# Order edges that hold each half piece of H behind the attention step traced before it

## The chip, the cores and the metric

The kernel runs on one core of a Trainium2 chip. The metric is the device time of one execution in microseconds (us), lower is better; times are medians of several runs, and one execution more is recorded by the profiler. Five engines run their own queues of instructions, each in order: TensorE (PE), VectorE (DVE), ScalarE (ACT), GpSimd (POOL) and SyncE (SP), which issues most DMAs. An instruction whose input or buffer is not ready holds up everything behind it on its engine.

## The reference

Three stages follow each other: attention with 32 global and 512 local tokens per batch (4 batches, 8 heads, head size 64, a window of 32 to either side, and all global tokens), a two-layer network with leaky ReLU on its 2176 rows (512 to 2048 to 512), and a soft mixture of 8 experts with 4 slots each.

```python
def _attn_ref(q_l, k_l, v_l, q_g, k_g, v_g):
    ...
    s_g = scale * np.matmul(q_g, k_all.transpose(0, 1, 3, 2))
    out_g = np.matmul(sm(s_g), v_all)
    s_ll = scale * np.matmul(q_l, k_l.transpose(0, 1, 3, 2))
    mask = np.abs(pos[:, None] - pos[None, :]) <= window
    s_ll = np.where(mask, s_ll, -1000000000.0)
    s_lg = scale * np.matmul(q_l, k_g.transpose(0, 1, 3, 2))
    s_l = np.concatenate([s_lg, s_ll], axis=-1)
    out_l = np.matmul(sm(s_l), np.concatenate([v_g, v_l], axis=2))

def _moe_ref(x, w_in, w_out):
    h = x @ w_in
    g = np.maximum(0.01 * h, h)
    return g @ w_out

def _moe2_ref(x, phi, w1, w2):
    logits = x @ phi
    d = softmax(logits, axis=0)
    slot_input = d.T @ x
    # expert e: relu(slot_input[e] @ w1[e]) @ w2[e]
    return softmax(logits, axis=1) @ slot_out
```

## The kernel before

The 2176 rows are 17 tiles of 128: tiles 0 to 15 are the local rows of the four batches, the last the global rows. Attention runs over 16 pairs of heads (batch b, pair i). A pair has these steps on PE: `a_T` turns k and q (`kTp`, `qTp`, emptied by ACT into `kT`, `qT`; DVE spreads `kT` into windows `kw`); `a_S` makes 32 score blocks `sc`, DVE adds the mask and takes maxima (`se`, `mx`, `nmx`), ACT takes eight exponentials with their sums; `a_E` turns them (`etp`, emptied by DVE into `eT`); `a_V` multiplies by the window values `vw` (`po`), and DVE writes `xn`. `g_S`, `g_E` and `g_V` (`gl`, `gg`, `get`, `geg`, `gpo`, `gxt`) do the global rows once per batch. The PSUM banks named `tp` (two) are shared by `kTp`, `qTp`, `etp`, `xtp`, `get`, `gg` and others, those named `sc` (two) by the scores.

A tile t of the network has these steps: `b_X` turns a tile of `xn` (`xtp`) into a high part `xxh` (ACT) and a rest `xxl` (DVE); `b_H` multiplies by a quarter f of `w_in` in twelve matmuls of 128x512 into a bank `hp` (two banks `hb`), which ACT empties into `g`. A half piece of H is six of the twelve. For the tiles of `BLK` (4 to 14) `blocks` then turns `g` in blocks of 32 on DVE (`gb`), and after two quarters moves 16 sub-blocks back into place: for f = 0, 1 all on POOL, for f = 2, 3 six on POOL, five on DVE and five on ACT (`MOVE`, L712). `b_M` makes logits `lg`, `b_D1` to `b_D3` the softmax pieces (`lp`, `nm`, `al`, `st`, `d`, `cm`, `ce`, `cs`, `cnat`), and `b_U` adds the slot inputs up (`up`, `uacc`; for tiles under 7 `up` sits in a bank of `hb`).

From tile 4 on, `b_items` lists the pieces of H of tile t among the later steps of tile t - 1, and `merge` deals attention's steps and these items out in proportion to the weights that stand with them. That is the order of the text. The order within an engine's queue is set by a scheduler that takes ready instructions by modelled times, so a piece of H can stand ahead of attention steps that are earlier in the text. `tc.issue_after(ins)` adds an edge of order: what the block traces on the engine of `ins` stands behind `ins` in that engine's queue. Before the change `behind` uses it for four half pieces of a tile, behind a step of the softmax (`ms["b"]`).

Of the kernel before, what the change touches and what calls it, by code (L numbers as in the profile page):

```python
# [20 lines left out]
def kernel(  # L21
# [15 lines left out]
    nc = tc.nc  # L37
# [4 lines left out]
    P = 128  # L42
# [3 lines left out]
    NQ = FF // 512  # L46
# [12 lines left out]
    def bank(tag, name, bufs):  # L59
        return ps.tile([P, 512], F32, tag=tag, name=name, bufs=bufs)  # L60

    def tp(name):
        return bank("tp", name, 2)
# [10 lines left out]
    ident = identr.bitcast(F32)  # L74
# [8 lines left out]
    def warm(t):  # L83

        nc.tensor.matmul(
            t, identr, identr.unsqueeze(1).to_broadcast([P, 4, P]), start=True, stop=True
        )
# [289 lines left out]
    xn = {}  # L377
    xb = []
    exp_last = [None]

    def a_T(b, i):
        qn, kn = nat.pop(("qn", b, i)), nat.pop(("kn", b, i))
        for src, dst, nm, bf in ((kn, kT, "kT", 4), (qn, qT, "qT", 2)):
            pt = tp(nm + "p")
            if b == 0:
                warm(pt)
            for T in range(NT):
                nc.tensor.transpose(
                    pt[:, P * T:P * T + P], src[:, T].rearrange("p h d -> p (h d)"), ident
                )  # L390
            t = sa.tile([P, S], F32, tag=nm, name=nm, bufs=bf)
            nc.scalar.activation(  # L392
                out=t, in_=pt, func=AF.Copy, scale=scale if nm == "qT" else 1.0,
            )
            dst[b, i] = t
        kt = kT[b, i]
        HW = NW // 2
        kwin[b, i] = []
        for hf in range(2):
            kw = sa.tile([P, HW, P], F32, tag="kw", name="kw", bufs=3)  # L400
            src = kt[:, 32 * HW * hf:32 * HW * hf + 96]
            src = bass.AP(src.tensor, src.offset, [src.ap[0], [32, HW], [1, 96]])
# [13 lines left out]
    def a_S(b, i):  # L416
        qt, kw = qT.pop((b, i)), kwin.pop((b, i))
        mx = sa.tile([P, 2, NT], F32, tag="mx", name="mx", bufs=2)
        nmx = sa.tile([P, 2, NT], F32, tag="nmx", name="nmx", bufs=2)
        sm = sa.tile([P, NT, 2], F32, tag="sm", name="sm", bufs=2)  # L420
        rs = sa.tile([P, NT, 2], F32, tag="rs", name="rs", bufs=2)
        es = []
        bks = [bank("sc", f"sc{e}", 2) for e in range(2)]
        if b == 0:
            for bk in bks:
                warm(bk)
        seq_ = [(T, u, e) for T in range(NT) for u in range(4) for e in range(2)]
        for T, u, e in seq_ if b > 1 else sorted(seq_, key=lambda x: x[2]):
            U = 4 * T + u
            if True:  # L430
                if True:
                    nc.tensor.matmul(  # L432
                        bks[e][32 * u:32 * u + 32, P * T:P * T + P],
                        qt[64 * e:64 * e + 64, 32 * U:32 * U + 32],
                        kw[win(U) // (NW // 2)][64 * e:64 * e + 64, win(U) % (NW // 2), :],
                        start=True, stop=True,
                    )
        for e in range(2):
            bk = bks[e]
            s = sa.tile([P, S + SG], F32, tag="se", name="se", bufs=4)[:, 0:S].rearrange(  # L440
                "p (t k) -> p t k", t=NT
            )
            for T in range(NT):
                nc.vector.tensor_tensor_reduce(  # L444
                    out=s[:, T, :], in0=bk[:, P * T:P * T + P],
                    in1=mask[:, 0 if T == 0 else 2 if T == NT - 1 else 1, :],
                    scale=1.0, scalar=-3.0e38, op0=ALU.add, op1=ALU.max,
                    accum_out=mx[:, e, T:T + 1],
                )
            nc.vector.tensor_scalar_mul(nmx[:, e], mx[:, e], -1.0)  # L450
            for T in range(NT):
                exp_last[0] = nc.scalar.activation(  # L452
                    out=s[:, T, :], in_=s[:, T, :], func=AF.Exp,
                    bias=nmx[:, e, T:T + 1], accum_out=sm[:, T, e:e + 1],
                ).ins
            es.append(s)
        nc.vector.tensor_scalar_add(sm, sm, 1e-9)
        nc.vector.reciprocal(rs, sm)
        sc[b, i] = (es, rs)
# [3 lines left out]
    def a_E(b, i):  # L463
        es, rs = sc[b, i]
        ets = []
        for e in range(2):
            pt = tp("etp")
            if b == 0:
                warm(pt)
            for T in range(NT):  # L470
                nc.tensor.transpose(pt[:, P * T:P * T + P], es[e][:, T, :], ident)  # L471
            et = sa.tile([P, S], F32, tag="eT", name="eT", bufs=2)
            (nc.vector.tensor_copy if b or e else nc.scalar.copy)(et, pt)
            ets.append(et)
        eT[b, i] = ets

    def a_V(b, i):
        ets = eT.pop((b, i))
        _, rs = sc.pop((b, i))
        vw = vwin.pop((b, i))  # L480
        po = bank("po", "po", 1)
        if b == 0:
            warm(po)
        pov = po.rearrange("p (t e d) -> p t e d", t=NT, e=2)
        for T in range(NT):
            for e in range(2):
                for u in range(4):
                    U = 4 * T + u
                    nc.tensor.matmul(  # L489
                        pov[32 * u:32 * u + 32, T, e, :],  # L490
                        ets[e][:, 32 * U:32 * U + 32],
                        vw[:, win(U), e, :],
                        start=True, stop=True,
                    )
        if i == 0:
            xn[b] = (xb[0] if b % 2 else xa).tile([P, NT, H, D], F32, tag="xn", name="xn", bufs=1)
        nc.vector.tensor_tensor(
            out=xn[b][:, :, 2 * i:2 * i + 2, :], in0=pov,
            in1=rs.unsqueeze(3).to_broadcast([P, NT, 2, D]), op=ALU.mult,
        )  # L500
# [168 lines left out]
    def b_H(t, f, half=None):  # L669
        xh, xl = xt[t]  # L670
        if half != 1:
            if f == 0:
                gt[t] = (
                    xa.tile([P, FF], F32, tag="xn", name="gx", bufs=1) if t in (3, NTT - 1)
                    else sa.tile([P, FF], F32, tag="vw", name="g2", bufs=2) if t == 2
                    else sb.tile([P, FF], F32, tag="g", name="g", bufs=2)
                )
            hps[0] = hb("hp")
        hp = hps[0]
        w = wi[f]  # L680
        lo, hi = {None: (0, KD), 0: (0, KD // 2), 1: (KD // 2, KD)}[half]
        for k in range(lo, hi):
            for n, (a, c) in enumerate(((xh, 0), (xh, 1), (xl, 0))):
                nc.tensor.matmul(  # L684
                    hp, a[:, k, :], w[c][:, k, :],
                    start=(k == 0 and n == 0), stop=(k == KD - 1 and n == 2),
                )
        if half == 0:
            return
        gs = gt[t][:, 512 * f:512 * f + 512]  # L690
        nc.scalar.activation(out=gs, in_=hp, func=AF.Prelu, alpha=0.01)  # L691
        if t in BLK:
            blocks(t, f, gs)
# [186 lines left out]
    def behind(item):  # L880
# [2 lines left out]
                item[1]()  # L883
        return (item[0], go) + item[2:]

    def b_items(t0, t1):
        its = []
        for t in range(t0, t1):
            li = l_items(t - 1)
            h = [(1.3, lambda t=t, f=f, a=a: b_H(t, f, a)) for f in range(NQ) for a in range(2)]  # L890
            x = [(0.5, lambda t=t: b_X(t + 1), t + 1)] if t + 1 < NTT else []
            if t - 1 in BLK:
                its += h[0:2] + [li[1]] + h[2:4] + [li[2]] + x + [behind(h[4])]
                its += [li[3]] + [behind(x) for x in h[5:8]] + [li[4], li[5]]
                continue
            its += h[0:2] + [li[0]] + h[2:4] + [li[1]] + h[4:5] + x + h[5:6]
            its += [li[2], h[6], li[3], h[7], li[4], (0.0, lambda: None), li[5]]
        return its
# [19 lines left out]
    t = wp.tile([P, 4, NT, 2, D], F32, tag="w", name="qk")  # L918
# [155 lines left out]
    held = loads.pop(0)  # L1074
# [75 lines left out]
    pt = tp("sitp")  # L1150
# [86 lines left out]
    for m, (c0, c1) in enumerate(((0, 256), (256, 384), (384, 512))):  # L1237
# [25 lines left out]
        for n, ts in enumerate(order2):  # L1263
# [63 lines left out]
```

## Time and profile before

| what | value |
|---|---|
| runs | 519.48, 517.45, 514.94 us |
| median | 517.45 us |
| the profiled execution | 516.28 us |
| its span, first to last instruction | 514.2 us |
| mean granted clock of PE, of full speed | 0.962 |
| PE busy | 464.5 us |
| DVE, ACT, POOL busy | 301.2, 248.7, 181.1 us |

The profiled execution has 2.08 us around its span and lies 1.17 us under the median. Busy time of PE contains matmuls at either clock. Idle time counts where the engine is the one that others wait for.

### The profile page before, as it was taken

To read this page: it belongs to the slowest core of one execution; us is meant where nothing else is said; L and a number is where in the kernel's file an instruction comes from. 1 tells how busy PE (TensorE), PEld (TensorE's weight loads), DVE (VectorE), ACT (ScalarE), POOL (GpSimd) and SP (SyncE) were. 2 spreads that over 40 slices of the span, in tenths; PEclk is the share of its full clock that TensorE was granted. 3 is DMA by queue.
4 is the path that set the end of the run, shared out by engine and by line. 5 is a ranking of instruction groups with operands and counts; after the bars stand their busy time and mean duration, and the time that the engine had idled before them with its cause. 6 is when DMAs were issued, how large, how long until landed. Compare 5 with 4: busy or idle time off the path is not lost.

```text
span 514.2 us, 13727 instructions
## 1 busy us (share of the span) xinstructions
PE 464.5 (90%) x5279; PEld 322.2 (63%) x5279; DVE 301.2 (59%) x996; ACT 248.7 (48%) x762; POOL 181.1 (35%) x345
## 2 busy tenths in 40 slices
PE   8976988978999989689898899999999999999994
PEld 5644766556775657456675667677777777633353
DVE  4586769759576663866766975656555541312422
ACT  4787878759654163444525473144433442300222
POOL 2066688443202015206263636516656620000000
PEclk9978899979998999879999999999999999999998
DMA  9998767799755750602480500229620059999987
GB/s 178 235 231 229 212 216 297 209 303 275 189 116 107 169 114 1 131 8 56 127 149 9 108 8 0 84 83 399 256 83 2 0 196 342 385 378 377 302 249 207
DMA packets 122397, 90.25 MB, mean 176 GB/s; under 512 B 75804, under 2 KB 101212, under 8 KB 122332
## 3 DMA queue, kind: packets, MB, share of 16 engines
q1 hardware_dynamic: 119660, 88.33, 60.2%
q10 hardware_dynamic: 2672, 1.05, 0.8%
q8 instruction: 41, 0.67, 0.6%
q14 instruction: 24, 0.20, 0.1%
HBM read 76.68 MB, written 8.65 MB: 166 GB/s over the span
## 4 chain that ended last, share of the span: by engine, by line
PE 60%; DVE 13%; ACT 7%; DMA 5%; issue 3%; POOL 2%; SPq 0%; ACTq 0%; POOLq 0%; DVEq 0%
PE hp L684 29%; PE ehp L1167 3%; PE up L805 3%; PE lg L735 3%; ACT se L452 2%; PE gtp L721 2%; PE sc L432 2%; DMA rraw<-in_moe_w_out_dram 2%; DVE se L444 2%; DMA rraw<-in_moe_w_in_dram 2%; PE po L489 2%; PE sop L1243 1%; POOL wn L259 1%; PE etp L471 1%; PE sop L1221 1%
## 5 line engine op out<-in xcount | busy, mean ns | idle before, releaser
L684 PE MATMUL hp<-wi,xxh 128*128 128x512 f32 x512 | 166.5, 407 | 7.1 <-ACT g L691 3.6
L712 POOL COPY g<-gb 32x256 f32<-32x256 f32 x242 | 97.6, 403 | 95.8 <-DVE gb L703 37.5
L684 PEld LDWEIGHTS hp<-wi,xxh 128*128 128x128 f32 x512 | 92.8, 191 | 41.2 <-issue 12.0
L684 PE MATMUL hp<-wi,xxl 128*128 128x512 f32 x256 | 101.5, 397 | 0.0
L452 ACT ACTIVATE se<-se,nmx 128x128 f32<-128x128 f32 x128 | 49.6, 390 | 24.2 <-DVE nmx L450 21.4
L691 ACT ACTIVATE g<-hp 128x512 f32<-128x512 f32 x60 | 35.7, 594 | 47.6 <-PE hp L684 46.9
L684 PEld LDWEIGHTS hp<-wi,xxl 128*128 128x128 f32 x256 | 48.7, 190 | 12.1 <-issue 0.8
L703 DVE STREAM_TRANSPOSE gb<-g 128x512 f32<-128x512 f32 x44 | 30.9, 706 | 19.4 <-ACT g L691 19.0
L200 POOL COPY vw<-vw 32x1664 f32<-32x1664 f32 x10 | 15.7, 1574 | 70.1 <-DMA vw<-in_v_g_dram 39.2
L259 POOL TENSOR_TENSOR wn<-wn,rraw 128x256 int32<-128x256 int32 x32 | 26.3, 836 | 32.6 <-DMA rraw<-in_moe_w_in_dram 23.4
L432 PE MATMUL sc<-kw,qT 64*32 64x128 f32 x1024 | 29.3, 292 | 1.1 <-issue 0.7
L444 DVE CUSTOM_DVE_ANT_0 se<-sc,mask 128x128 f32<-128x128 f32 x128 | 28.7, 282 | 1.4 <-PE sc L432 1.2
L471 PE MATMUL etp<-identr,se 128*128 128x128 f32 x128 | 23.1, 301 | 5.3 <-ACT kT L392 4.0
L259 POOL TENSOR_TENSOR wo<-wo,rraw 128x256 int32<-128x256 int32 x23 | 18.1, 800 | 25.5 <-DMA rraw<-in_moe_w_out_dram 4.5
L712 ACT COPY g<-gb 32x256 f32<-32x256 f32 x55 | 22.1, 402 | 9.2 <-DVE cs L788 4.1
L489 PE MATMUL po<-vw,eT 128*32 128x64 f32 x1024 | 24.0, 227 | 2.4 <-DMA vw<-vw 1.5
L249 ACT ACTIVATE rraw<-rraw 128x256 int32<-128x256 uint32 x55 | 23.2, 435 | 5.9 <-DMA rraw<-in_moe_w_in_dram 5.1
L432 PEld LDWEIGHTS sc<-kw,qT 64*32 64x32 f32 x1024 | 20.2, 112 | 7.7 <-issue 4.0
L403 DVE COPY kw<-kT 128x672 f32<-128x672 f32 x32 | 19.2, 638 | 9.0 <-ACT kT L392 8.8
L759 ACT ACTIVATE st<-lg,nm 128x128 f32<-128x128 f32 (+1 forms) x16 | 6.0, 373 | 38.2 <-DVE nm L758 34.5
L489 PEld LDWEIGHTS po<-vw,eT 128*32 128x32 f32 x1024 | 18.4, 113 | 9.7 <-issue 7.3
L452 ACT ACTIVATION_READ_ACCUMULATOR se<-se,nmx 128x1 f32 x128 | 24.1, 188 | 0.0
(227 smaller groups left out, 818.1 us busy)
## 6 DMA issues: line engine op xcount, KB each, us to landing
ew<-in_moe_w_dram SPq DMA_DIRECT2D x23, 1024.0 KB, 8.6
rraw<-in_moe_w_in_dram SPq DMA_DIRECT2D x32, 256.0 KB, 3.6
vw<-in_v_l_dram SPq DMA_DIRECT2D x60, 112.0 KB, 3.5
rraw<-in_moe_w_out_dram SPq DMA_DIRECT2D x23, 256.0 KB, 5.3
ew<-in_moe_w_dram SPq DMA_DIRECT2D x9, 512.0 KB, 9.6
ew<-in_moe_w_dram SPq DMA_DIRECT2D x17, 256.0 KB, 5.6
wo_f<-wo SPq DMA_DIRECT2D x16, 256.0 KB, 3.4
vn<-in_v_l_dram SPq DMA_DIRECT2D x4, 1024.0 KB, 6.1
```

The lines of the kernel that those rows point to most:

```text
L249: nc.scalar.activation(out=m, in_=lo, func=AF.Copy, scale=2.0 ** -29)
L259: nc.gpsimd.tensor_tensor(out=di, in0=di, in1=m, op=ALU.add)
L403: nc.vector.tensor_copy(kw[:, :, 0:96], src)
L432: nc.tensor.matmul(bks[e][32 * u:32 * u + 32, P * T:P * T + P], qt[64 * e:64 * e + 64, 32 * U:32 * U + 32], kw[win(U) // (NW // 2)][64 * e ...
L444: nc.vector.tensor_tensor_reduce(out=s[:, T, :], in0=bk[:, P * T:P * T + P], in1=mask[:, 0 if T == 0 else 2 if T == NT - 1 else 1, :], sca ...
L452: exp_last[0] = nc.scalar.activation(out=s[:, T, :], in_=s[:, T, :], func=AF.Exp, bias=nmx[:, e, T:T + 1], accum_out=sm[:, T, e:e + 1],).ins
L471: nc.tensor.transpose(pt[:, P * T:P * T + P], es[e][:, T, :], ident)
L489: nc.tensor.matmul(pov[32 * u:32 * u + 32, T, e, :], ets[e][:, 32 * U:32 * U + 32], vw[:, win(U), e, :], start=True, stop=True,)
L684: nc.tensor.matmul(hp, a[:, k, :], w[c][:, k, :], start=(k == 0 and n == 0), stop=(k == KD - 1 and n == 2),)
L691: nc.scalar.activation(out=gs, in_=hp, func=AF.Prelu, alpha=0.01)
L703: nc.vector.transpose(out=gb[:, f % 2], in_=gs)
L712: copy(dst[32 * c:32 * c + 32, :, a], src[32 * a:32 * a + 32, :, c])
```

## The change

Every instruction of `a_T`, `a_S`, `a_E` and `a_V` on PE leaves its handle in `last_a`, so that `last_a` is the last matmul of attention traced so far. A helper `held` wraps each half piece of H that `b_items` lists (tiles 4 to 14, quarters 0 to 3, both halves): when the piece is traced, its matmuls get an edge behind that matmul. Pieces that `behind` wraps keep that edge too. The work itself, the buffers and the order of the text stay as they are.

```diff
     exp_last = [None]
+    last_a = [None]
...
-                nc.tensor.transpose(
+                last_a[0] = nc.tensor.transpose(
                     pt[:, P * T:P * T + P], src[:, T].rearrange("p h d -> p (h d)"), ident
-                )
+                ).ins
...
+    def held(item):
+        def go():
+            with tc.issue_after(last_a[0]):
+                item[1]()
+        return (item[0], go)
+
     def b_items(t0, t1):
         its = []
         for t in range(t0, t1):
             li = l_items(t - 1)
-            h = [(1.3, lambda t=t, f=f, a=a: b_H(t, f, a)) for f in range(NQ) for a in range(2)]
+            h = [held((1.3, lambda t=t, f=f, a=a: b_H(t, f, a))) for f in range(NQ) for a in range(2)]
```

The same `last_a[0] =` stands at the matmuls of `a_S`, `a_E` and `a_V`. The listing of the queues is the same on PE up to the `up` of tile 2 (190.31 us in the trace of before) and again behind attention's last score step, apart from small swaps.

First place, PE behind the `up` of tile 2, where tile 4's H begins. Before, the row ahead of these ends a run of 36 matmuls of H (`hp`); `etp` is the turn of exponentials, `lg` the logits of tile 3, `kTp` and `qTp` the next pair's k and q:

```order
L684 MATMUL hp<-wi,xxl 128x512
L471 MATMUL etp<-identr,se 128x128 x4
L735 MATMUL lg<-gT,pmat 32x128
L471 MATMUL etp<-identr,se 128x128 x4
L735 MATMUL lg<-gT,pmat 32x128 x7
L684 MATMUL hp<-wi,xxh 128x512 x2
```

After, the row ahead of these ends a run of 18:

```order
L687 MATMUL hp<-wi,xxl 128x512
L472 MATMUL etp<-identr,se 128x128 x4
L738 MATMUL lg<-gT,pmat 32x128 x4
L472 MATMUL etp<-identr,se 128x128 x4
L687 MATMUL hp<-wi,xxh 128x512 x2
L687 MATMUL hp<-wi,xxl 128x512
```

Before, 12 more matmuls of H follow, then `kTp`, `po`, `qTp`, `gtp` and the scores. After, 6 follow, then the same, 12 of H, and the scores; 12 stand behind the scores, at the second place.

Second place, PE behind those scores, before:

```order
L735 MATMUL lg<-gT,pmat 32x128 x8
L471 MATMUL etp<-identr,se 128x128 x8
L750 MATMUL lg<-lp,s_77 128x128
L388 MATMUL kTp<-identr,kn 128x128 x4
L388 MATMUL qTp<-identr,qn 128x128 x4
L471 MATMUL etp<-identr,se 128x128 x4
```

And after:

```order
L738 MATMUL lg<-gT,pmat 32x128 x8
L687 MATMUL hp<-wi,xxh 128x512 x2
L687 MATMUL hp<-wi,xxl 128x512
L687 MATMUL hp<-wi,xxh 128x512 x2
L687 MATMUL hp<-wi,xxl 128x512
L472 MATMUL etp<-identr,se 128x128 x8
L687 MATMUL hp<-wi,xxh 128x512 x2
L687 MATMUL hp<-wi,xxl 128x512
L687 MATMUL hp<-wi,xxh 128x512 x2
L687 MATMUL hp<-wi,xxl 128x512
L753 MATMUL lg<-lp,s_77 128x128
L389 MATMUL kTp<-identr,kn 128x128 x4
```

Two half pieces of H have moved in, on both sides of `etp`. On ACT at the same place (`g_3180<-gb` are the turning copies of tile 4, `xxh` that of tile 5), before:

```order
L660 ACTIVATE xxh<-xtp 128x512
L712 COPY g_3180<-gb 32x8x32 x2
L452 ACTIVATE se,sm<-se,nmx 128x128 x4
L712 COPY g_3180<-gb 32x8x32 x3
L452 ACTIVATE se,sm<-se,nmx 128x128 x4
L392 ACTIVATE kT<-kTp 128x512
L759 ACTIVATE st,zt<-lg,nm 128x128
L392 ACTIVATE qT<-qTp 128x512
```

And after:

```order
L663 ACTIVATE xxh<-xtp 128x512
L453 ACTIVATE se,sm<-se,nmx 128x128 x8
L694 ACTIVATE g<-hp 128x512
L393 ACTIVATE kT<-kTp 128x512
L762 ACTIVATE st,zt<-lg,nm 128x128
L767 ACTIVATE al<-al 128x1
L393 ACTIVATE qT<-qTp 128x512
L715 COPY g_3180<-gb 32x8x32 x5
```

The five turning copies have moved behind the exponentials, `kT` and `qT`, and an eviction of H has come in ahead of `kT`.

Third place, ACT at the last two score steps of attention, beside tile 7, before:

```order
L691 ACTIVATE g<-hp 128x512
L392 ACTIVATE kT<-kTp 128x512
L392 ACTIVATE qT<-qTp 128x512
L392 ACTIVATE kT<-kTp 128x512
L392 ACTIVATE qT<-qTp 128x512
L452 ACTIVATE se,sm<-se,nmx 128x128 x16
```

And after:

```order
L453 ACTIVATE se,sm<-se,nmx 128x128 x8
L694 ACTIVATE g<-hp 128x512
L393 ACTIVATE kT<-kTp 128x512
L694 ACTIVATE g<-hp 128x512
L393 ACTIVATE qT<-qTp 128x512
L393 ACTIVATE kT<-kTp 128x512
L453 ACTIVATE se,sm<-se,nmx 128x128 x8
L393 ACTIVATE qT<-qTp 128x512
L453 ACTIVATE se,sm<-se,nmx 128x128 x8
```

The first eight exponentials of the sixteen have moved ahead of the second `qT`.

## Rows read from the trace of the kernel before

**Rows 1.** The page: span, and busy time of the engines.

```profile
span 514.2 us, 13727 instructions
PE 464.5 (90%) x5279; PEld 322.2 (63%) x5279; DVE 301.2 (59%) x996; ACT 248.7 (48%) x762; POOL 181.1 (35%) x345
```

**Rows 2.** Stretches: length, busy time of each engine, granted clock, DMA share, GB/s.

```profile
191.30:210.00 18.70, 18.70 (x224) 14.53 (x220) 8.00 (x16) 7.52 (x23) 7.89 (x17) 1.00 0.19 42
210.00:216.00 6.00, 3.52 (x39) 2.36 (x34) 5.92 (x24) 2.06 (x10) 1.40 (x1) 0.99 0.40 80
216.00:220.00 4.00, 0.14 (x1) 0.14 (x2) 3.18 (x11) 3.95 (x17) 2.53 (x7) 0.50 0.58 131
220.00:226.00 6.00, 6.00 (x79) 2.88 (x79) 4.34 (x29) 1.10 (x6) 0.00 (x0) 0.50 0.01 3
...
255.00:264.00 9.00, 8.45 (x199) 6.28 (x198) 6.21 (x13) 3.77 (x11) 5.02 (x12) 1.00 0.43 84
...
278.00:300.00 22.00, 19.59 (x374) 14.30 (x374) 16.75 (x66) 13.20 (x56) 9.99 (x18) 1.00 0.37 67
...
345.00:400.00 55.00, 55.00 (x375) 41.11 (x373) 31.67 (x85) 21.89 (x59) 34.07 (x86) 1.00 0.50 188
```

**Rows 3.** PE in order of time, 208 to 220: start, us, instruction, [idle before <- releaser].

```profile
208.75 0.66 PE L654 MATMUL xtp<-identr,xn 128*128 128x128 f32 x4
...
210.11 0.65 PE L735 MATMUL lg<-gT,pmat 128*32 128x128 f32 x16
...
219.86 1.11 PE L471 MATMUL etp<-identr,se 128*128 128x128 f32 x4 [4.05 <-ACT kT L392]
```

**Rows 4.** The chain that ended last, 201 to 215: start, us, what.

```profile
201.70 2.95 PE hp L684 x12
...
214.78 1.65 ACT se L452 x8
```

**Rows 5.** ACT in order of time, 213 to 220.

```profile
213.95 0.81 ACT L712 COPY g<-gb 32x256 f32<-32x256 f32 x2 [3.91 <-DVE nmx L450]
...
216.44 1.23 ACT L712 COPY g<-gb 32x256 f32<-32x256 f32 x3
...
219.23 0.57 ACT L392 ACTIVATE kT<-kTp 128x512 f32<-128x512 f32 x1
```

**Rows 6.** PE in order of time, the longest other waits, 248 to 283.

```profile
248.80 1.06 PE L805 MATMUL up<-g,d 128*32 128x512 f32 x8 [1.62 <-DVE d L782]
...
277.80 0.73 PE L684 MATMUL hp<-wi,xxh 128*128 128x512 f32 x2 [1.18 <-DVE uacc L810]
...
282.59 0.66 PE L388 MATMUL kTp<-identr,kn 128*128 128x128 f32 x4 [1.07 <-DVE eT L473]
```

**Rows 7.** DVE in order of time, 210 to 275.

```profile
210.07 0.69 DVE L661 SCALAR_TENSOR_TENSOR xxl<-xtp,xxh 128x512 fp32r<-128x512 f32 x1 [1.11 <-ACT xxh L660]
...
212.37 0.71 DVE L703 STREAM_TRANSPOSE gb<-g 128x512 f32<-128x512 f32 x1
...
216.42 2.09 DVE L712 COPY g<-gb 32x256 f32<-32x256 f32 x5
...
219.84 1.02 DVE L403 COPY kw<-kT 128x672 f32<-128x672 f32 x2 [0.31 <-ACT kT L392]
220.78 0.47 DVE L404 COPY kw<-kgT 128x224 f32<-128x224 f32 x2
...
271.88 3.19 DVE L712 COPY g<-gb 32x256 f32<-32x256 f32 x5
```

**Rows 8.** POOL in order of time, the window copy at 272.

```profile
272.03 1.57 POOL L200 COPY vw<-vw 32x1664 f32<-32x1664 f32 x1 [4.06 <-DMA vw<-in_v_g_dram]
```

More of the change, by code (lines that the diff above doesn't have):

```diff
@@ L431, in a_S @@
                 if True:
-                    nc.tensor.matmul(
+                    last_a[0] = nc.tensor.matmul(
                         bks[e][32 * u:32 * u + 32, P * T:P * T + P],
@@ L436, in a_S @@
                         start=True, stop=True,
-                    )
+                    ).ins
         for e in range(2):
@@ L470, in a_E @@
             for T in range(NT):
-                nc.tensor.transpose(pt[:, P * T:P * T + P], es[e][:, T, :], ident)
+                last_a[0] = nc.tensor.transpose(
+                    pt[:, P * T:P * T + P], es[e][:, T, :], ident
+                ).ins
             et = sa.tile([P, S], F32, tag="eT", name="eT", bufs=2)
@@ L488, in a_V @@
                     U = 4 * T + u
-                    nc.tensor.matmul(
+                    last_a[0] = nc.tensor.matmul(
                         pov[32 * u:32 * u + 32, T, e, :],
@@ L493, in a_V @@
                         start=True, stop=True,
-                    )
+                    ).ins
         if i == 0:
```

## The prediction

> **What bounds the kernel now.** I read the page first: TensorE (PE) is busy 464.5 of a span of 514.2 us, VectorE (DVE) 301.2 and ScalarE (ACT) 248.7 [rows 1]. The kernel is PE's, but 50 us of PE are idle, so the question is where. The stretches tell it [rows 2]: 191.3 to 210.0 is full, 210 to 220 has PE busy 3.52 and 0.14 of 10, and 345 to 400 is full again without a gap. Only the order between about 191 and 325 is changed, so only what PE loses there can be won; behind it the reader sees PE at 55.00 of 55.00, and what is won early is passed on to the end one for one.
>
> Three kinds of loss stand there. **First**, the hole at tile 4: 2.48 idle in 210 to 216 and 3.86 in 216 to 220 [rows 2], 6.34 together, 4.05 of it in one wait before the transposes `etp` at 219.86 [rows 3]. It is named as a wait for ACT's `kT`: `etp` needs the PSUM bank that ACT empties with the `kT` copy at 219.23, and ahead of that copy stand, in ACT's queue, five turning copies (0.81 and 1.23) and eight exponentials [rows 4, 5]. **Second**, the clock: the granted clock is 0.50 through 216 to 226, the lower of its two levels, 1.2 of 2.4 GHz, after a stretch in which PE was busy 3.52 of 6 us; the 6.00 us of busy PE in 220 to 226 ran at that level [rows 2]. **Third**, shorter waits: 1.62 for `d` at 248.80, 1.18 for `uacc` at 277.80, 1.07 for `eT` at 282.59 [rows 6]. Why the hole exists is seen at 191.3 to 210.0: PE runs all 48 matmuls of H of tile 4 before the score step, and has none left to lay into the waits of it.
>
> **The change, part by part.** No instruction is added or taken away; matmuls of H change places on PE, and what hangs on them on the other engines follows. I compare the same position in the work before and after, so that a moved matmul costs nothing by itself: only idle time and the clock count.
>
> (a) *The hole.* At the score step that follows `xtp` at 208.75, 36 matmuls of H instead of 48 stand ahead; twelve cost 2.95 [rows 4]. So `xtp` comes at 205.8, `xxl` (1.32 behind it before [rows 3, 7]) at 207.1, and the eight maskings of scores end where the first turn `gb` starts, 2.30 behind `xxl` [rows 7]: 209.4. With that `gb` (0.71) and two short copies the negated maxima are there at 210.4. ACT's order is now eight exponentials at once, without the five copies: four with their sums take 1.65 [rows 4], eight 3.3, to 213.7; then one eviction of H and `kT`, some 0.55 each [rows 5]: `etp` starts at 214.85. PE gets there by 213.5: the scores end at 207.15 (210.11 less 2.95) [rows 3], 3.4 of work follows (the 3.52 busy us of 210 to 216 begin 0.11 before it) [rows 2], and the twelve matmuls of H that now lie between, 2.95. Idle 1.35 in place of 6.34: **5.0 won**.
>
> (b) *The clock.* If PE does not stand still for long, the 6.14 busy us of 216 to 226 [rows 2] are some 3.1: **3.0 won**. The bounds are 0 (it falls all the same) and 3.1.
>
> (c) *New waits behind it.* The next scores need `kw`, built by DVE after `kT` and after the second turn `gb`, which now has moved ahead of it: 1.02 for two windows and half of 0.47 [rows 7], to 216.3, where PE is ready at 215.45: 0.9. Then `up` needs `d`, and DVE's order now has the five turning copies (2.09) [rows 7] ahead of `d`: PE is there at 218.0, `d` at 219.2: 1.1. **2.0 lost**; the bounds are 0, since PE may come later than the bare durations say, and 3.1, if the copies take the 3.19 they took at 271.88 [rows 7].
>
> (d) *Tile 5.* The wait of 1.62 for `d` [rows 6] goes: `d` moves ahead of the turning copies on DVE there, and six matmuls of H, `etp` and nine scores stand behind it on PE. A wait of some 0.45 of `po` for its bank (`xn`, behind eight maskings) comes in: **1.2 won**.
>
> (e) *Tile 6.* Here H no longer helps: six of its matmuls move behind the scores, and between the last scores and `gxt` DVE does a `get` copy, two `gb`, eight maskings, `xxl` and the `kw` windows. By the rows 0.7 + 1.4 + 1.7 + 0.69 + 1.49 [rows 7], 6 us, against about 3.4 of PE's own work: `qTp` waits for the bank that `xxl` reads, `gxt` for `xg`, 2.6 together, and `up` 0.45 more. The same stretch, 255 to 264, idles 0.55 before [rows 2]: **2.5 lost**, with 0 and 3.5 as bounds.
>
> (f) *Tile 7, first half.* Twelve matmuls of H go from before `etp` to behind `kTp`: they stand where PE now waits 1.18 and 1.07 [rows 6]. I leave 0.4, since `uacc` is still behind the turning copies: **1.85 won**.
>
> (g) *Tile 7, second half.* `qTp` waits for the second `eT`, behind two `gb` and eight maskings on DVE: 1.75. The last scores wait for `qT`, which ACT's order now has behind eight exponentials (3.3) where it stood ahead of sixteen before: PE fills 1.55 with `xtp` and `po`, and waits 1.75. Of the 2.41 idle in 278 to 300 [rows 2], 1.07 is in (f) and 0.71 stays; 0.63 goes off: **2.9 lost**, between 0 and 3.5.
>
> Sum: -5.0 - 3.0 + 2.0 - 1.2 + 2.5 - 1.85 + 2.9 = **-3.65**. SP's loads of `qn` and `vw` swap by a place or two and POOL's window copy `vw` stands earlier among its turning copies; both have microseconds in hand, and cost nothing by these rows.
>
> One row deserves a rule. DVE's five turning copies took 2.09 at 216.42 and 3.19 at 271.88, where POOL's window copy of 1.57 ran at 272.03 [rows 7, 8]. The Trainium skill, "SBUF — State Buffer", section "Who interferes with whom", says that VectorE and GpSimd share one port pair, under an exclusive lock, so that one blocks the other for a whole instruction; the trace agrees with it in that row (1.1 longer). By the rule a window copy that now meets the negated maxima of (a) would hold them by up to 1.57, and the sum would be -2.1; without it, -3.65.
>
> The profiled execution took 516.28: its span and 2.08 around it. It lies 1.17 under the median of 517.45. From it the sum gives 512.6, from the median 513.8; I say **513.5**.
>
> **The rivals.** *The waits shrink.* The terms (c), (e) and (g) set bare durations of DVE and ACT against bare durations of PE; if PE comes a little later than I let it, each wait is shorter by as much and the path no longer. With half of their 7.4 gone the sum is -7.35, 510.1 from the median. For it: waits of (c), (e), (g) are all of 0.9 to 1.75, of the size of my errors. Against: each stands behind an in-order queue in the listing.
>
> *The clock falls more often: slower.* The change thins H out where attention runs, and three stretches without any H remain, each of 8 to 12 us with 2.6 to 3.5 idle: the scores to `up` of tile 4, (e) and (g). In 212 to 216, half idle, such a stretch ended in a granted clock of 0.50 [rows 2]; against it speaks 278 to 300, 2.41 idle, at 1.00. A fall costs 3.0, as in (b). One gives -0.65, two +2.35, 519.8, and only with the third it is slower by over 1%: +5.35, 522.8. "TensorE: Matmul & The Clock Gate" in the Trainium skill, section "Part 1: The HAM clock gate", says of the array's clock that "the default state is throttled, and activity releases the throttle"; rows 2 agree with that.
>
> *The edges do not bite.* If attention's chain through ACT and DVE (scores, maskings, exponentials, transposes) set the pace, H would only move the idle time: 517 to 518. The listing speaks against it: the edges did change the order, and the hole's chain shortens by the five copies and 2.95.
>
> **How the numbers follow.** The forecast, -1 to -5.2, has 0.50 (512.3 to 516.5); the shrinking waits 0.31 (507.5 to 512.3); the clock 0.12 (517 to 523), of which a good half is over 1%; edges without effect 0.07. 1% (5.2 us) is what a measurement of this kernel can tell from no change. Faster by over 1%: the shrinking waits and a little of the forecast, 0.36. Slower by over 1%: 0.08. Within: 0.56. The range, 508.5 to 520, takes in half to three quarters of the waits on one side and two falls of the clock on the other.
>
> **What would show it.** In the changed profile: the idle time before `etp` of (a) under 2 us and no stretch at 0.50 near it; waits of `up` for `d`, of `gxt` for `xg`, of `sc` for `qT`. The forecast is wrong if PE idles over 15 us between 191 and 325, if the clock falls twice there, or if 345 to 400 gains gaps.

## The result and the profile after

| kernel | runs | median us | lowest to highest | mean granted clock |
|---|---|---|---|---|
| before, beside it | 20 | 517.00 | 513.48 to 526.23 | |
| changed | 20 | 520.19 | 515.71 to 525.82 | 0.956 |

The ratio is 1.0068 (95%: 1.0039 to 1.0097): slower, where 513.5 was forecast. Two later sets of the same order (below, e1 and e4) give 1.0013 and 1.0012, and neither is clear of no change by itself. Ratios leave disturbed runs out and medians keep them, so with this scatter I also give the difference of the two means of a set, all runs taken: +2.4, +1.3 and +2.0 us. Taken together the change costs some 2 us, and it was to win 3.65.

The stretches of the changed kernel, with the columns of [rows 2]:

```profile
193.60:210.00 16.40, 16.38 (x190) 11.58 (x192) 8.61 (x18) 7.82 (x26) 7.71 (x16) 1.00 0.41 77
208.00:216.00 8.00, 8.00 (x118) 6.21 (x116) 5.42 (x26) 3.29 (x13) 3.85 (x7) 1.00 0.46 59
216.00:220.00 4.00, 1.81 (x41) 1.03 (x39) 2.59 (x7) 3.95 (x15) 1.49 (x4) 1.00 0.58 131
220.00:224.00 4.00, 3.86 (x44) 1.41 (x43) 3.26 (x14) 1.41 (x5) 1.14 (x3) 0.57 0.01 4
255.00:262.00 7.00, 4.89 (x129) 3.42 (x126) 6.62 (x27) 3.13 (x12) 3.51 (x6) 1.00 0.58 117
262.00:264.40 2.40, 1.64 (x52) 1.13 (x52) 1.08 (x5) 1.77 (x10) 2.19 (x6) 1.00 1.30 195
264.40:268.00 3.60, 3.60 (x34) 2.29 (x30) 0.29 (x1) 0.00 (x0) 2.51 (x7) 0.53 0.65 87
278.00:300.00 22.00, 19.24 (x375) 14.15 (x374) 14.90 (x64) 12.67 (x55) 10.12 (x19) 1.00 0.35 67
345.00:400.00 55.00, 55.00 (x376) 41.09 (x375) 31.27 (x84) 21.64 (x57) 32.83 (x83) 1.00 0.52 192
```

And its PE in order of time, the ups and the waits that answer to [rows 3, 6]:

```profile
193.62 1.06 PE L808 MATMUL up<-g,d 128*32 128x512 f32 x8 [1.73 <-DVE d L785]
218.11 0.66 PE L472 MATMUL etp<-identr,se 128*128 128x128 f32 x4 [1.93 <-ACT kT L393]
222.78 1.41 PE L808 MATMUL up<-gx,d 128*32 128x512 f32 x8
245.27 1.07 PE L808 MATMUL up<-g,d 128*32 128x512 f32 x8
262.76 0.33 PE L591 MATMUL gxt<-identr,xg 128*128 128x128 f32 x1 [2.87 <-DVE xg L586]
275.06 1.07 PE L808 MATMUL up<-g,d 128*32 128x512 f32 x8 [0.93 <-DVE d L785]
293.21 1.05 PE L433 MATMUL sc<-kw,qT 64*32 64x128 f32 x56 [2.18 <-ACT qT L393]
304.83 1.06 PE L808 MATMUL up<-g,d 128*32 128x512 f32 x8 [1.17 <-DVE cm L788]
322.86 1.06 PE L808 MATMUL up<-g,d 128*32 128x512 f32 x8
345.36 1.06 PE L808 MATMUL up<-g,d 128*32 128x512 f32 x8
```

What to see: the hole is gone as forecast (208 to 216 is full, 1.93 is left before `etp` where 4.05 stood), but the clock still falls behind it (0.57 in 220 to 224), and a second time behind a new wait of 2.87 for `xg` (0.53 in 264.4 to 268.0, with PE fully busy). Before, that place and everything from 226.1 to 345 ran at 1.00. Idle time did go down, so it is not what made the kernel slower: from the `up` of tile 2 to that of tile 7 PE idles 10.1 us (129.24 less 119.13) where it idled 12.5:

```profile
190.31:320.64 130.33, 117.84 (x1530) 84.17 (x1531) 86.66 (x302) 62.38 (x219) 54.38 (x114) 0.96 0.29 60
```

```profile
193.62:322.86 129.24, 119.13 (x1531) 83.79 (x1531) 86.64 (x302) 61.83 (x219) 54.73 (x114) 0.97 0.30 60
```

The starts of `up` cut the changed region into six stretches that can be compared between kernels whatever came before them (each number is a difference of two such starts; "up 2" is the `up` of tile 2):

| profile | up 2 at | up 2-3 | 3-4 | 4-5 | 5-6 | 6-7 | 7-8 | sum |
|---|---|---|---|---|---|---|---|---|
| before | 190.31 | 34.06 | 24.43 | 23.13 | 30.97 | 17.74 | 21.84 | 152.2 |
| e5_before | 188.09 | 34.05 | 24.48 | 23.15 | 30.76 | 17.74 | 21.84 | 152.0 |
| changed | 193.62 | 29.16 | 22.49 | 29.79 | 29.77 | 18.03 | 22.50 | 151.7 |
| e1_again | 191.72 | 31.52 | 24.00 | 29.25 | 30.34 | 18.03 | 22.46 | 155.6 |
| e4_not6 (same order) | 190.65 | 29.66 | 22.10 | 30.18 | 30.35 | 18.07 | 22.49 | 152.9 |
| e2_tile4 | 187.97 | 31.21 | 23.47 | 24.43 | 32.96 | 17.91 | 22.05 | 152.0 |
| e3_tile6 | 193.94 | 34.13 | 23.63 | 24.91 | 34.22 | 17.37 | 21.86 | 156.1 |
| e7_tile5 | 190.23 | 34.05 | 22.63 | 23.91 | 36.11 | 17.74 | 21.82 | 156.3 |
| e11_tiles45 | 188.13 | 29.71 | 22.11 | 29.04 | 30.31 | 18.04 | 22.04 | 151.3 |
| e16_tiles7on | 187.60 | 35.61 | 23.61 | 23.15 | 30.65 | 17.78 | 22.15 | 153.0 |
| e12_one_quarter | 195.00 | 31.72 | 24.31 | 23.59 | 33.42 | 17.36 | 22.02 | 152.4 |
| e6_gxt_later | 188.63 | 31.28 | 22.46 | 27.37 | 32.42 | 18.03 | 22.49 | 154.1 |
| e8_act_copies | 190.72 | 32.60 | 26.65 | 23.83 | 35.55 | 17.37 | 22.04 | 158.0 |
| e9_fill_before | 191.76 | 32.71 | 22.59 | 26.10 | 34.83 | 17.38 | 21.83 | 155.4 |
| e13_fill5 | 188.69 | 29.58 | 22.14 | 29.17 | 29.57 | 18.07 | 22.51 | 151.0 |
| e15_tiles45_fill5 | 187.58 | 29.86 | 22.15 | 29.25 | 30.39 | 18.03 | 22.05 | 151.7 |
| e10_fill_after | 192.04 | 31.21 | 21.51 | 28.37 | 29.49 | 17.74 | 23.33 | 151.7 |
| e14_fill8_again | 192.13 | 30.39 | 21.53 | 28.40 | 28.84 | 17.75 | 21.89 | 148.8 |
| e17_tiles45_fill8 | 198.46 | 31.04 | 21.52 | 26.92 | 30.38 | 17.74 | 21.83 | 149.4 |

The first column is a warning: up to there all these kernels have the same order on PE, and it still ends anywhere from 187.6 to 198.5. The 3.3 us that the first profile of the changed kernel lay behind before at that point were scatter, and a span alone would have misled. Where a first stretch is 1 to 2 us longer than its like (e1, e2, e6, e10, e14, e16, e17), the clock fell right behind the `up` of tile 2, as the windows below show for e1.

### The profile page after: what moved, and what is told of

It reads as the page before. It is cut to its first block, busy times and chain, and to the rows that moved or that the text cites. A ratio compares the mean times of both kernels' runs of the same rounds, so it can differ in the third digit from the quotient of the medians.

```text
span 517.6 us, 13727 instructions
## 1 busy us (share of the span) xinstructions
PE 467.9 (90%) x5279; PEld 322.2 (62%) x5279; DVE 299.9 (58%) x996; ACT 247.7 (48%) x762; POOL 181.4 (35%) x345
## 3 DMA queue, kind: packets, MB, share of 16 engines
q10 hardware_dynamic: 2672, 1.05, 0.8%
## 4 chain that ended last, share of the span: by engine, by line
PE 61%; DVE 9%; DMA 8%; ACT 5%; issue 2%; SPq 2%; POOL 1%; ACTq 0%; POOLq 0%; DVEq 0%
PE hp L687 31%; PE up L808 3%; PE ehp L1176 3%; PE lg L738 3%; PE po L492 2%; PE sc L433 2%; DVE se L445 2%; ACT se L453 2%; DMA rraw<-in_moe_w_in_dram 2%; PE gtp L724 2%; DMA vn<-in_v_l_dram 2%; PE sop L1230 1%; DMA vw<-in_v_l_dram 1%; PE gpo L578 1%; DMA ew<-in_moe_w_dram 1%
## 5 line engine op out<-in xcount | busy, mean ns | idle before, releaser
L433 PE MATMUL sc<-kw,qT 64*32 64x128 f32 x1024 | 30.4, 292 | 2.5 <-ACT qT L393 2.4
```

The costliest lines, as they stand in the source:

```text
L433: last_a[0] = nc.tensor.matmul(bks[e][32 * u:32 * u + 32, P * T:P * T + P], qt[64 * e:64 * e + 64, 32 * U:32 * U + 32], kw[win(U) // (NW / ...
```

## The experiments

Ratios are to the kernel before in the same set, with 95% in brackets; a sum is that of the table above.

**The changed kernel again**, for its own scatter (no edit).

> The changed kernel once more, with a second profile. Theory A (the order gives the gain back): the front, up to the up of tile 2, is the same code as before and ends again near 190.3 us; the first profile's 193.6 was scatter; then the stretch from there to the up of tile 8 (151.7 in the first profile, 152.2 before) comes out near 155, and the ratio at 1.004 to 1.010. Theory B (the loss is in the front): the up of tile 2 is again 2 to 4 us late, and the stretch behind it stays at 151 to 153.

Measured: 518.68, ratio 1.0013 (0.9970 to 1.0056), means +1.3; sum 155.6 at 191.72. The sum is theory A's (near 155), the ratio is not (1.004 to 1.010), and the third profile of this order (e4, 152.9) lies in theory B's 151 to 153: one profile does not settle it. The two profiles run one program; their first two stretches differ by 3.9 us, and the windows show why. The changed kernel's first profile behind `up` of tile 2 and tile 3, then the same in this one:

```profile
195.00:199.00 4.00, 4.00 (x19) 3.12 (x18) 2.94 (x7) 3.11 (x14) 1.58 (x1) 1.00 0.00 0
222.80:226.90 4.10, 4.10 (x36) 1.74 (x36) 3.53 (x24) 1.53 (x8) 0.00 (x0) 0.91 0.00 0
```

```profile
193.00:197.00 4.00, 4.00 (x12) 3.10 (x12) 1.48 (x5) 2.12 (x12) 1.10 (x1) 0.57 0.00 0
223.20:227.30 4.10, 4.06 (x13) 2.03 (x14) 3.52 (x24) 1.47 (x8) 0.00 (x0) 0.50 0.00 0
```

12 matmuls where 19 ran, 13 where 36 ran: the clock makes nearly all of the 3.9 us between two executions of one program.

**The kernel before again** (no edit).

> The kernel before once more, for a second profile. Theory A (the stretches between the ups of the tiles belong to the order, and the front scatters): the front, up to the up of tile 2, ends anywhere from 186 to 194 us, and the stretches behind it repeat within 0.8 us: 34.1, 24.0, 23.1, 31.0, 17.7, 21.8, with the clock at 0.50 behind the hole of tile 4. Theory B (single profiles cannot be told apart there either): a stretch differs by over 2 us from the first profile.

Measured: 514.01 in one run; every stretch within 0.21 us of the first profile, the hole again 4.04 with the clock at 0.50 behind it:

```profile
208.00:213.70 5.70, 3.29 (x34) 2.25 (x32) 5.70 (x24) 1.95 (x8) 1.41 (x1) 1.00 0.38 74
213.70:217.60 3.90, 0.00 (x0) 0.00 (x0) 3.01 (x10) 3.85 (x17) 2.52 (x7) 0.51 0.59 134
217.60:223.90 6.30, 6.27 (x79) 3.03 (x79) 4.63 (x29) 1.35 (x7) 0.00 (x0) 0.50 0.01 3
```

Theory A. The order before is stable in this region; the order after is not.

**Edges on one group of tiles.** All with this edit in place of the changed line of `b_items`, with other conditions for `t == 4`:

```diff
+            h = [(1.3, lambda t=t, f=f, a=a: b_H(t, f, a)) for f in range(NQ) for a in range(2)]
+            if t == 4:
+                h = [held(x) for x in h]
```

Tile 4 alone:

> Edges on the pieces of tile 4 alone. Theory A: the hole before etp is filled as in the changed kernel (-4.9 between the ups of tiles 2 and 3, -1.9 up to that of tile 4) and nothing takes it back at tile 6: some 5 us under before, 512, ratio about 0.990. Theory B: the front is late here too, or the gain is absorbed behind it: within 2 us of before.

Measured: 516.20, ratio 1.0001 (0.9966 to 1.0036), sum 152.0. The first stretch wins 2.9; the fourth loses 2.0, the third 1.3. Theory B: absorbed behind it, without any edge at tile 6.

Tile 6 alone:

> Edges on the pieces of tile 6 alone. Theory A: the wait of gxt for xg (2.87 in the changed kernel) and the clock that falls behind it stand here without the gain of tile 4: 3 to 6 us over before, ratio 1.006 to 1.012. Theory B: within 1 us of before, as before it can wait for the same chain.

Measured: 520.12, ratio 1.0069 (1.0031 to 1.0107), sum 156.1: theory A's size, but at another place: the wait of `gxt` is 0.89, and the fourth stretch (+3.3) carries the loss.

All tiles but 6 (`t != 6`):

> Edges on all tiles but 6. Theory A: the gain of tile 4 stays and the loss of tile 6 (6.7 between the ups of tiles 4 and 5, some 1.6 of it moved work) goes: 3 to 6 us under the changed kernel, so 1 to 4 under before. Theory B: as the changed kernel, 2 to 4 us over before.

Measured: 518.68, ratio 1.0012 (0.9968 to 1.0056). The order is that of the changed kernel on every engine: the edges of tile 5 hold tile 6 as well, since the pieces of H follow each other through two banks. So it says nothing on tile 6, and is a third profile of the changed kernel.

Tile 5 alone:

> Edges on the pieces of tile 5 alone. Theory A (thinning H at tile 5 and 6 is the loss): the first stretch stays at 34, the third goes from 23.1 to 27 to 30 us, and the kernel is 3 to 6 us slower than before, ratio 1.006 to 1.012. Theory C (PE only runs into DVE's pace because it comes early): with the hole of tile 4 still there PE is not early, the third stretch stays under 25 us, ratio 0.998 to 1.004.

Measured: 520.62, ratio 1.0068 (1.0034 to 1.0101), sum 156.3. Theory A's size, but the third stretch stays at 23.9 and the fourth goes from 31.0 to 36.1, where the last scores idle and the clock falls behind:

```profile
293.00:297.00 4.00, 1.89 (x28) 0.65 (x26) 3.55 (x22) 0.52 (x4) 1.18 (x1) 1.00 0.82 130
297.00:301.00 4.00, 4.00 (x18) 1.91 (x14) 0.63 (x2) 3.05 (x16) 1.57 (x1) 0.57 0.01 4
```

Tiles 4 and 5 (`t < 6`):

> Edges on tiles 4 and 5 alone: the changed kernel's order up to the up of tile 7, then that of before but for small swaps. The fifth and sixth stretch, 18.03 and 22.50 in all three profiles of the changed kernel, are 17.74 and 21.84 again (0.95 less) if the swaps of tile 7 and 8 cost them; the first four add up to 111 to 115 as in the changed kernel. Rival: they stay at 18.0 and 22.5, and something carried along from tiles 4 to 6 costs them. Ratio to before 0.998 to 1.005.

Measured: 515.39, ratio 0.9979 (0.9953 to 1.0005), means -0.9. Of the 0.65 that the changed kernel adds in the sixth stretch (7-8) 0.45 goes. The fifth (6-7) stays at 18.04, but up to the `up` of tile 7 the order is still that of the changed kernel, so this run does not test it.

Tiles 7 to 14 (`t >= 7`):

> Edges on tiles 7 to 14 alone. The changed kernel against edges on tiles 4 and 5 alone was 519.1 to 516.2 in the mean. If the edges from tile 7 on cost that, this kernel is 1 to 3 us over before, with stretches five and six at 18.0 and 22.5 and the first four as in before; ratio 1.001 to 1.006. Rival: they cost only where attention comes early, ratio 0.998 to 1.001.

Measured: 516.28, ratio 1.0010 (0.9978 to 1.0041); 17.78 and 22.15 in stretches five and six (17.74 and 21.84 before). The rival: alone they cost nothing that can be told in the time. Up to the `up` of tile 7 its order is that of before, and its second stretch, with the clock up from end to end, takes 23.61 where before takes 24.43.

One half piece of tile 4:

```diff
+            if t == 4:
+                h = [held(x) if n in (3,) else x for n, x in enumerate(h)]
```

> Only one half piece of tile 4 held (quarter 1, second half): four matmuls of H come into the hole instead of eighteen, and the order of tiles 5 and 6 stays as before up to the scores of the last pairs. If the losses behind tile 4 come from the order dealt anew, the first stretch falls by 0.9 to 2 us, the second and third stay at 24.4 and 23.1, and the time is 1 to 2 us under before, ratio 0.996 to 0.999. Rival: what is won at the hole is taken back by the chains of attention whatever the order: stretches two to four grow by as much, ratio 1.000 to 1.003.

Measured: 518.84, ratio 1.0055 (1.0025 to 1.0085). The first stretch falls by 2.3, the second and third stay, and the fourth grows by 2.5, where the order was dealt anew. The gain at the hole came, but the time lies outside both ranges: neither foresaw a loss behind it of that size.

**The transpose `gxt` behind four half pieces of H**, on the changed kernel: `g_V` of batch 2 keeps it back, and `b_H` traces it with an edge.

```diff
+        while late and half is not None:
+            with tc.issue_after(h_ins):
+                late.pop()()
```

> The changed kernel with the transpose gxt held behind the fourth half piece of H of tile 6. Theory A (the wait of gxt for xg, 2.3 to 3.2 us, and the clock that falls behind it are what gives the gain back): the stretch between the ups of tiles 4 and 5 (29.2 to 30.2) shrinks by 3 to 4.5 us and the time falls to some 514 to 515, ratio to before 0.994 to 0.999. Theory C (DVE sets the pace of that stretch): the wait comes back in front of the next step that needs DVE (xtp, etp or up), the stretch shrinks by under 1 us, ratio 1.000 to 1.006.

Measured: 519.34, ratio 1.0008 (0.9973 to 1.0043). Its PE at that place:

```profile
258.60 0.84 PE L433 MATMUL sc<-kw,qT 64*32 64x128 f32 x34 [1.61 <-ACT qT L393]
266.55 0.27 PE L592 MATMUL gxt<-identr,xg 128*128 128x128 f32 x1
269.74 1.07 PE L819 MATMUL up<-g,d 128*32 128x512 f32 x8 [1.44 <-DVE d L796]
```

The wait of `gxt` is gone, and scores and `up` wait instead; the third stretch wins 2.4, with the clock up from end to end, and the fourth loses 2.3. The time is theory C's, the stretch lies between the two theories. Part of the wait belongs to attention's chain through ACT and DVE, not to `gxt`; whether the loss of the fourth stretch is that chain's or the new order's (it was dealt anew from `gxt` on) is not shown.

**ACT's five turning copies of tile 4 behind the next `kT`**, on the kernel before, H untouched:

```diff
+            if t == 4 and MOVE[f // 2][n] == "A":
+                pend.append(args)
...
+            if nm == "kT":
+                with tc.issue_after(ins):
+                    for args in pend:
+                        nc.scalar.copy(*args)
+                pend.clear()
```

> The kernel before with only ACT's five turning copies of tile 4 moved behind the next kT copy; H stays where it was. Step (a) of the prediction counted both a chain without the five copies (2.0 us) and twelve matmuls less ahead (2.95). If that is right, the wait before etp falls by 2.0 us, the hole from 6.3 to some 4.3, and the clock still falls; 1 to 2.5 us under before, ratio 0.995 to 0.998. Rival: the hole is set by the scores and maskings, and the copies were hidden: hole over 5.8 us, ratio 0.998 to 1.002.

Measured: 520.57, ratio 1.0058 (1.0020 to 1.0096). The wait before `etp` falls from 4.05 to 2.77 and the first stretch by 1.5, the clock falls all the same, and stretches two and four lose 2.2 and 4.6. (a) counted the copies rightly in direction, 1.3 where 2.0 was expected; the time is outside both ranges, by the stretches behind.

**Matmuls that compute nothing in the hole of the kernel before** (extra work whose results are not used):

```diff
+        if (b, i) == (2, 3):
+            with tc.issue_after(q_last[0]):
+                for _ in range(14):
+                    warm(bks[0])
```

> The kernel before with 14 matmuls that compute nothing (identity, 128x512, into the first score bank) between qTp and etp, in the hole of tile 4, H where it was. Term (b) of the prediction, the clock: if the clock falls because PE stands still there, the stretch between the ups of tiles 2 and 3 falls from 34.05 by some 3 us to 31, with no 0.50 behind it. Rival: the low clock comes from the small matmuls ahead of the hole as well, it falls all the same, and the stretch stays within 0.8 us. Behind it the order is dealt anew by the scheduler, and the later stretches may lose 2 to 5 us as in the runs so far; the time is between 0.994 and 1.008.

Measured: 520.22, ratio 1.0041 (1.0011 to 1.0071). The clock holds, and from `etp` to `up` takes 3.15 us (221.32 to 224.47) where it took 4.51 before (219.86 to 224.37):

```profile
218.00:222.00 4.00, 3.12 (x15) 2.11 (x13) 3.12 (x10) 3.97 (x16) 1.97 (x5) 1.00 0.55 125
222.00:226.00 4.00, 3.59 (x77) 1.95 (x78) 3.19 (x21) 0.56 (x4) 0.00 (x0) 1.00 0.01 4
```

So standing still in the hole is what brings the clock down there, but in that stretch it costs 1.36 and not 3; some 0.8 more lies behind `up`, up to 226.1 where the fall ends (24.43 before, 23.61 in e16). The new order loses 6.8 in stretches three and four.

**Eight such matmuls in the changed kernel**, in the wait left before `etp`:

> The changed kernel with 8 such matmuls in the wait that is left before etp at tile 4. If that wait brings the clock down at 217 to 220 us, the fall goes and the first two stretches together take 51 to 52 us in this profile, with no 0.50 in them; rival: the clock falls there all the same, 51.5 to 55.5 as in the three profiles of the changed kernel. The later stretches as in the changed kernel or 2 us to either side; ratio 0.998 to 1.008.

Measured: 511.88, ratio 0.9877 (0.9840 to 0.9914), clock 0.968 over the timed runs. Faster than both kernels, by more than any theory gave. Again:

> The kernel with eight such matmuls once more, for a second profile and a second set of times. If its 511.9 holds, the ratio is again 0.984 to 0.992 and the profile ends near 510, with less low clock than the first profile's, which lay over its median; rival: the first set was a lucky chip, and the ratio is 0.995 to 1.003.

Measured: 511.28, ratio 0.9889 (0.9857 to 0.9921), sum 148.8. It holds. The wait is closed, and the clock stays up:

```profile
216.00 2.09 PE L85 MATMUL sc<-identr 128*128 128x512 f32 x8
217.93 0.60 PE L478 MATMUL etp<-identr,se 128*128 128x128 f32 x4
218.77 0.45 PE L439 MATMUL sc<-kw,qT 64*32 64x128 f32 x16 [0.24 <-ACT qT L395]
```

```profile
214.00:222.50 8.50, 7.19 (x96) 5.10 (x95) 6.64 (x20) 6.72 (x27) 4.17 (x7) 1.00 0.28 64
272.40:301.20 28.80, 26.37 (x407) 18.43 (x407) 21.54 (x82) 15.09 (x55) 12.10 (x24) 1.00 0.27 51
```

But eight of them also make the scheduler deal the order behind anew. **Five** leave every other instruction on every engine in its place:

> The changed kernel with five matmuls that compute nothing in the wait before etp at tile 4, where it had eight in the run before this one; with five every other instruction on every engine keeps the place it has in the changed kernel. If the clock behind that wait is what makes the changed kernel slow, the first two stretches lose their 0.50 behind etp (217 to 220 us) and take 50.5 to 51.5 us, the clock's mean over the timed runs rises, and the time falls by 2 us or more under the changed kernel's 519, ratio to before below 1.000. If the 511.9 came from the order dealt anew behind it, the time stays at 518 to 520, ratio 1.001 to 1.007.

Measured: 516.36, ratio 0.9998 (0.9968 to 1.0029), means +0.3, clock 0.964; 1.12 is left before `etp` and the clock stays up:

```profile
213.60 0.66 PE L478 MATMUL etp<-identr,se 128*128 128x128 f32 x4 [1.12 <-ACT kT L395]
218.27 1.06 PE L814 MATMUL up<-gx,d 128*32 128x512 f32 x8 [1.08 <-DVE d L791]
```

```profile
211.00:214.00 3.00, 1.88 (x12) 1.31 (x10) 1.23 (x4) 3.00 (x15) 0.13 (x1) 1.00 0.65 148
214.00:218.30 4.30, 2.95 (x76) 1.52 (x75) 4.14 (x13) 2.47 (x6) 2.51 (x6) 1.00 0.10 23
218.30:224.00 5.70, 5.70 (x102) 3.12 (x103) 3.81 (x25) 3.14 (x17) 0.00 (x0) 1.00 0.00 0
```

Same order, PE only kept busy: the loss of 1.3 to 2.4 us is gone, outside the interval of the first set of the changed kernel, though not outside those of the two later ones. Between five and eight lie another 4.8 us by the medians. The fill at `etp` holds the clock with either, so the order behind is the likely cause. In e14's profile 3.0 of it stand in the five stretches behind the `up` of tile 3 (118.4 against 121.5 in e13, one fall of the clock in either), in e10's profile 1.0; the rest is not shown.

The same on tiles 4 and 5 alone, with five and with eight:

> Edges on tiles 4 and 5 alone (515.4, ratio 0.998) with five such matmuls in the wait before etp, order otherwise unchanged. If the fill spares a fall of the clock, 1.5 to 3 us under the kernel with edges on tiles 4 and 5, ratio to before 0.991 to 0.996. Rival: the clock falls as before or elsewhere, ratio 0.996 to 1.000.

Measured: 515.32, ratio 0.9978 (0.9946 to 1.0010): as without the fill. The clock held there in the profile without it too.

> Edges on tiles 4 and 5 alone with eight matmuls that compute nothing in the wait before etp: up to the up of tile 7 the order of the kernel that took 511.3 and 511.9. If the edges from tile 7 on cost 1 to 3 us of their own, 508.5 to 511, ratio to before 0.982 to 0.988. Rival: they cost nothing here (alone they cost nothing: 1.001), and the ratio is 0.987 to 0.991.

Measured: 513.21, ratio 0.9935 (0.9895 to 0.9975): not under the 511.6 with all edges, and in neither range. So the edges from tile 7 on cost nothing here; why the changed kernel took some 519 and edges on tiles 4 and 5 alone 515.4 stays open. Its profile is of use all the same. Between the `up` of tile 4 and that of tile 5 it has the order of e14 on every engine, and no fall of the clock where e14 has one; e17 first, then e14:

```profile
251.02:277.94 26.92, 24.77 (x384) 17.66 (x381) 17.69 (x76) 13.07 (x50) 12.13 (x24) 1.00 0.53 115
```

```profile
244.05:272.45 28.40, 26.25 (x383) 18.64 (x380) 18.43 (x73) 12.45 (x49) 12.08 (x24) 0.94 0.51 109
```

The same work and the same 2.15 us of idle time: the fall costs 1.5 there (e10, the third profile of this order, takes 28.37 with it). The best version is the changed kernel with eight filling matmuls.

## Why the prediction was wrong

By its own steps, with the mean of the three profiles of the changed kernel (30.11, 22.86, 29.74, 30.15, 18.04, 22.48) against the first of before:

| steps | predicted | measured |
|---|---|---|
| (a), (b), (c): up 2-3 | -6.0 | -3.95 |
| (d): 3-4 | -1.2 | -1.57 |
| (e): 4-5 | +2.5 | +6.61 |
| (f), (g): 5-6 | +1.05 | -0.82 |
| nothing: 6-8 | 0 | +0.94 |
| sum | -3.65 | +1.21 |

The timed means say +1.3 to +2.4. The furthest off is (e), and it is so in each of the three profiles (+6.1 to +7.1); what it and (b) have in common is that they priced waits of PE without the clock behind them.

(a) **Right**: 1.93 to 2.28 left before `etp`, 1.35 forecast. The case of -2.1, POOL's window copy beside the negated maxima `nmx`, took for new what stood in the kernel before: there one of the two `nmx` took 1.18 beside that copy, and in the changed kernel both together take 0.54 (before, then changed):

```profile
214.60 1.57 POOL L200 COPY vw<-vw 32x1664 f32<-32x1664 f32 x1 [9.17 <-DMA vw<-in_v_l_dram]
215.02 1.18 DVE L450 TENSOR_SCALAR nmx<-mx 128x4 f32<-128x4 f32 x1
```

```profile
212.27 1.58 POOL L200 COPY vw<-vw 32x1664 f32<-32x1664 f32 x1 [1.79 <-DMA vw<-in_v_l_dram]
213.39 0.54 DVE L451 TENSOR_SCALAR nmx<-mx 128x4 f32<-128x4 f32 x2
```

(b) **Wrong in its mechanism.** It took the clock as won if PE does not stand still for long, and it did not stay up behind a wait of about 2 us: in six profiles with this wait unfilled (1.93 to 2.28: the first, e1, e2, e4, e6, e11) the clock fell behind it in four; with five or eight matmuls in it, in none of five. Its price was mis-sized too: 2.2 at the hole (1.36 by e9 and 0.8 by e16), not 3.0, as the work from `etp` to `up` doesn't halve at full clock (2.65 busy in 3.10 us) and short waits come up. (c) came as forecast where the clock holds, `up` waits 1.08 for `d` in e13; in the changed kernel the low clock hides that wait, and a profile with a short fall (29.66 and 22.10 in e4) is no slower than one without (29.71 and 22.11 in e11, the same order). The longer fall of e1, with the one behind the `up` of tile 2, cost the 3.9. Without e1, (a) to (d) came out at -6.8 and -6.7 for the forecast -7.2. That is in part luck: the fall that (b) left out hid the wait that (c) put in.

(d) **Right on the wait, the size by luck.** The 1.62 for `d` is gone. But 0.8 of what the stretch wins is the low clock that before still had behind `up` (e16), and the bare time of the scores that moved into the next stretch is another 0.8.

(e) **The step that failed.** +2.5 was forecast, up to 3.5, and +6.66 measured in the first profile. The waits are those forecast, `gxt` for `xg` 2.87 (2.33 and 3.24 in e1 and e4) and `up` for `d` 0.93, 3.80 where 3.05 was said. What the term put at nothing is the clock behind that wait: 3.60 us at 0.53 behind `gxt`, and a fall stands there in all six profiles with the changed order at this place (the first, e1, e4, e11, e13, e15). It costs some 1.5, taken over from e17 against e14, whose wait there is the scores' for `qT`. Another 1.6, by bare durations, is work moved in from both sides (scores, `etp`, `xtp`); that is no loss of the whole, as the stretches beside it win it. With the 0.55 that went, 3.80 + 1.5 + 1.6 - 0.55 = 6.35 of the 6.66.

(f), (g) **Half right.** `sc` waits 2.18 for `qT` (1.75 forecast), `qTp` 0.45 (1.75 forecast), the waits for `uacc` and `eT` are gone, and 0.8 of work moved out: about 0. `up` waits 1.17 for `cm`, where 0.38 stood (0.37 in e1 and e4, where the clock fell before it).

**Passed on one for one: right behind 345** (55.00 of 55.00; from the `up` of tile 8 to that of the last tile 104.85 us, 104.88 before), **wrong between**: stretches 6-7 and 7-8 cost 0.94. By e11 some 0.45 of it hangs on the edges from tile 6 on; what makes the 0.30 of 6-7 is not shown.

Of the rivals, the clock falling more often is nearest to what came: two falls gave 519.8 there, and 520.19 was measured. It got 0.12. The number is in part luck: its price of 3.0 a fall is not borne out (nothing to be seen at `etp`, 1.5 in (e), 0.7 in (g)). The row that I set against it, 2.41 idle of 22 us at 1.00 [rows 2], says little of another order: in the changed order one and the same wait of `sc` for `qT` (2.17 to 2.19) left the clock at 1.00 in two profiles (the first, e13) and brought it down in four (e1, e4, e11, e15), where stretch 5-6 takes 30.31 to 30.39 and not 29.57 or 29.77. In e1:

```profile
293.60:295.40 1.80, 0.73 (x53) 0.73 (x59) 0.93 (x3) 1.01 (x5) 1.63 (x5) 1.00 0.87 198
295.40:299.00 3.60, 3.60 (x54) 2.32 (x39) 2.72 (x20) 1.07 (x5) 2.18 (x3) 0.53 0.72 101
```

The shrinking waits did not come, and the edges did bite.

What the runs show: the stretch of tile 6 gives back what tile 4 wins, by longer waits and by the clock behind them; in e6, which moved the wait, another loss came up behind it. That alone brings the change to nothing won (0.9998 in e13, where the fall behind `gxt` is still there). The clock behind the wait left before `etp` is the best account of the rest, by e13, but of the profiles only e1's shows it as time. Open: some 0.8 of the 2 us is in none of the profiles' stretches, which is within the scatter of the timed sets, and only part of the 4.8 us with eight was found in the profiles.

## What to carry to other kernels

Price a wait on TensorE with the clock behind it, also one of 2 us, and ask whether a few idle matmuls can sit in it: five took back what moving the work had cost. Time them in the whole kernel, since 14 in the kernel before made it 4.2 us slower by the order dealt anew. A local gain in an order that a scheduler deals is worth little until the stretches behind it are looked at: single edits here made a later stretch 2 to 5 us longer (e2, e3, e7, e8, e12). Compare stretches between landmarks, in two profiles of the same program first; spans mix in what the front happened to do.

## What was not expected of the hardware

The front is the same program in all 19 profiles, and its end moves by 11 us, most of it with the granted clock: of the 10.9 between the two rows, 8.8 is busy time of PE. From 60 us to the `up` of tile 2, at the fastest and the slowest front (e15_tiles45_fill5, then e17_tiles45_fill8):

```profile
60.00:187.50 127.50, 115.35 (x1522) 82.39 (x1520) 94.49 (x322) 84.92 (x264) 48.35 (x55) 0.99 0.78 212
```

```profile
60.00:198.40 138.40, 124.14 (x1540) 90.10 (x1538) 95.42 (x329) 88.31 (x271) 52.12 (x58) 0.94 0.73 200
```

The mean clock of the timed runs goes with the time in most kernels: 0.961 before, 0.956 to 0.962 for the changed one, 0.968 and 0.969 with eight filling matmuls; but e9 was slower than before at 0.964; the waits of its stretches three and four are the likely cause. The Trainium skill, "TensorE: Matmul & The Clock Gate", section "Part 1: The HAM clock gate", has activity release the throttle; e13 agrees, where work without use kept the clock at 1.00 behind `etp` (0.964 over the timed runs, 0.956 to 0.962 without it) and the time fell.
